# Small-matmul bursts re-ordered in a fused attention and MLP kernel, with its q/k and v loads requested earlier

One core of a Trainium2 chip (trn2). The metric is the device time of one execution in microseconds, taken from several executions per kernel; lower is better.

## The reference, cut to what matters

```python
# q, k, v: (8, 8, 576, 64). Attention per batch and head, two branches added:
q_d, k_d, v_d = means of q, k, v over 4 neighbouring positions      # 144 positions
out_up    = repeat(softmax(q_d k_d^T / 8) v_d, 4)
out_local = softmax(q k^T / 8 where |i - j| < 4) v
x = (out_up + out_local) as (4608 tokens, 512)
# then the MLP:
h = x @ w_in            # 512 -> 2048
out = (h * sigmoid(1.702 h)) @ w_out     # 2048 -> 512
```

## The kernel before

The MLP runs in nine groups of 512 tokens: 64 dense matmuls for `w_in` (`mm1`), 64 for `w_out` (`mm2`), 512 columns each. The attention of batch g+1 runs beside the dense matmuls of group g, as bursts of small matmuls at numbered positions (0 to 79, four dense matmuls per position in `mm1`, one per position from 16 on). Below, "group 1 to 6" are the six groups with the regular positions `POS`; group 0 carries batch 1 at its own positions, groups 7 and 8 carry no attention. "AV" is the product of the scores' exponentials with v; a PSUM tile is a buffer that TensorE's results go to.

```python
POS = [13, 16, 33, 42, 53, 62, 71]
# 13: scores of heads 0-3 (s_pe(0))   16: their exponentials    33: scores of heads 4-7 (s1)
# 42: AV of head pairs 0, 1           53: AV of pairs 2, 3      62, 71: transposes back

def s_pe(qd):
    st["s", qd] = scores(b, qd)      # 80 matmuls, 32x64 tiles, 60 columns, two PSUM tiles
    st["d", qd] = scores_d(b, qd)    # 24 matmuls, 144 columns, the third PSUM tile

# the third blocks of the downsampled AV: two array tiles, and a filler in the other two
blocks = [(kc, x, 0) for kc in range(3) for x in range(2)]
blocks += [(0, 0, 1), (0, 1, 1), (1, 0, 1), (2, 0, 1)]     # (0, 1, 1) is the filler

# per group, in program order; GpSimd issues q/k loads and does pooling and casts itself
load_v4(b)                           # SyncE queue
prep_qk(b, 0); pool_qk(b, 0)         # VectorE transposes, GpSimd pooling
for qd in range(NQ): load_qk(b + 1, qd)     # GpSimd queue, f32 to bf16 on the way
prep_v(b, nc.gpsimd)                 # GpSimd cast of v, needs v of batch b
load_v(b + 1)                        # SyncE queue, after the cast
prep_qk(b, 1); pool_qk(b, 1); prep_v4(b, nc.gpsimd)
```

The softmax here doesn't subtract the row's maximum and nothing guards it: scores larger than these inputs give would overflow.

## Time and profile before

| | before |
|---|---|
| device time, median (range) | 324.07 us (323.53 to 325.09) |
| span of the profiled run | 321.3 us |
| granted TensorE clock, mean | 0.999 |
| groups 1 to 6, one undisturbed group | 33.4 us |

How to read it: the chain is the work that ended last, followed back from the end of the run; the granted clock is the share of its full clock that TensorE was given. TensorE is on the chain for nearly the whole span, so every pause of TensorE is added to the time. To see a burst's cost I take the time from the last dense weight load before it to the first dense weight load after it. In this measure the six bursts of an undisturbed group take 1.683, 1.747, 1.339, 1.340, 1.073 and 1.073 us (first scores, second scores, AV, AV, transposes, transposes). What a burst takes beyond its clean time (the changed bursts have clean times of their own, 1.60, 1.67, 1.26, 1.26, 1.05 and 1.05 us) is called a stop.

### The profile page before, as it was taken

What the parts mean: (1) busy time and instruction counts of PE and PEld (TensorE: products, weight loads), DVE (VectorE), ACT (ScalarE), POOL (GpSimd) and SP (SyncE); (2) the same over time, 40 slices, a digit from 0 to 9 for tenths busy, and PEclk for the clock granted to TensorE, in tenths of its full rate; (3) what the DMA queues carried; (4) which work ended last, traced back from release to release, by engine and by line L of the source; (5) the groups of instructions that cost most, each with busy time, mean ns of one, the idle gap of its engine ahead of it and who ended that gap; (6) DMA issues with size and microseconds to landing.
All of it is one profiled execution on the core that took longest, in us unless ns stands there. A gap on an engine that the chain in (4) does not pass through costs nothing.

```text
span 321.3 us, 10981 instructions
## 1 busy us (share of the span) xinstructions
PE 314.1 (98%) x4916; PEld 158.9 (49%) x4916; DVE 135.3 (42%) x224; ACT 183.9 (57%) x317; POOL 140.0 (44%) x172
## 2 busy tenths in 40 slices
PE   8999999999999999999999999999999999999995
PEld 3764555455444455455545554455445544444444
DVE  6973627802673076605770478036811650000000
ACT  4565762667456673668365936683677466415611
POOL 8992960299009920794059603980296000000000
PEclk9999999999999999999999999999999999999999
DMA  7999999899619941895169715991360110020011
GB/s 121 114 198 210 177 122 207 159 247 253 161 43 207 196 117 67 185 215 130 65 150 215 168 37 144 213 197 46 108 106 3 69 67 2 0 98 33 2 62 68
DMA packets 63550, 40.02 MB, mean 125 GB/s; under 512 B 44048, under 2 KB 54416, under 8 KB 63504
## 3 DMA queue, kind: packets, MB, share of 16 engines
q0 software_dynamic: 18864, 14.95, 32.4%
q1 hardware_dynamic: 44496, 24.32, 31.1%
q8 instruction: 38, 0.62, 0.9%
q14 instruction: 8, 0.07, 0.1%
q10 hardware_dynamic: 144, 0.07, 0.1%
HBM read 44.83 MB, written 9.44 MB: 169 GB/s over the span
## 4 chain that ended last, share of the span: by engine, by line
PE 94%; DVE 2%; DMA 2%; issue 1%; POOL 0%; ACT 0%; DVEq 0%; POOLq 0%
PE pm L687 37%; PE pm L743 36%; PE pa L373 4%; PE pa L743 2%; PE pa L687 2%; PE pa L487 2%; PE pa L392 2%; PE pa L434 2%; PE pa L456 2%; DMA qb<-in_q_dram 2%; PE pm L758 1%; PE pm L816 1%; DVE y L473 1%; PE pa L573 1%; PE pa L497 0%
## 5 line engine op out<-in xcount | busy, mean ns | idle before, releaser
L743 PE MATMUL pm<-w_out_bf,gT 128*128 128x512 bf16 x528 | 121.7, 380 | 0.0
L687 PE MATMUL pm<-xT,w_in_bf 128*128 128x512 bf16 x544 | 121.1, 379 | 0.0
L698 ACT ACTIVATE gT<-pm 128x512 bf16<-128x512 f32 x136 | 81.0, 598 | 44.6 <-PE pm L687 44.6
L687 PEld LDWEIGHTS <-w_in_bf 128*128 128x128 bf16 x576 | 55.6, 98 | 66.8 <-issue 0.4
L743 PEld LDWEIGHTS <-gT 128*128 128x128 bf16 x560 | 51.6, 98 | 59.1 <-issue 0.2
L417 DVE TENSOR_TENSOR es<-es,mask 128x600 bf16<-128x600 bf16 x28 | 20.2, 736 | 84.8 <-ACT es L403 83.9
L294 POOL TENSOR_TENSOR pq<-kT 128x576 f32<-128x576 bf16 x14 | 16.3, 1161 | 88.4 <-DVE kT L276 88.4
L728 ACT ACTIVATE osb<-pm 128x512 f32<-128x512 f32 (+2 forms) x35 | 20.8, 594 | 40.0 <-PE pm L743 35.6
L599 ACT COPY od<-pa 128x384 f32<-128x384 f32 (+1 forms) x56 | 18.5, 412 | 32.9 <-DVE y L473 15.0
L473 DVE TENSOR_TENSOR y<-pa,rc 128x896 bf16<-128x896 f32 x28 | 30.6, 1091 | 1.0
L620 DVE TENSOR_TENSOR xT<-pa,od 128x570 bf16<-128x570 f32 x28 | 21.1, 753 | 12.2 <-ACT od L599 10.8
L730 DVE TENSOR_SCALAR osb<-pm 128x128 f32<-128x128 f32 x1 | 0.3, 292 | 55.3 <-ACT osb L728 55.3
L314 POOL TENSOR_TENSOR v<-v 112x512 f32<-112x512 f32 x18 | 22.8, 1266 | 0.0
L276 DVE STREAM_TRANSPOSE kT<-kb 128x576 f32<-128x576 f32 x16 | 20.0, 1249 | 4.1 <-DMA kb<-in_k_dram 3.9
L403 ACT ACTIVATE es<-pa 128x600 bf16<-128x600 f32 x32 | 19.7, 667 | 2.7 <-PE pa L373 2.4
L276 DVE STREAM_TRANSPOSE qT<-qb 128x576 f32<-128x576 f32 x16 | 19.9, 1242 | 0.4
L230 POOL DMA_DIRECT2D vb<-in_v_dram x20 | 13.7, 696 | 6.6 <-DMA w_in_bf<-in_moe_w_in_dram 4.4
L409 ACT ACTIVATE ed<-pa 128x864 bf16<-128x864 f32 x16 | 14.4, 897 | 2.0 <-PE pa L392 1.8
L373 PEld LDWEIGHTS <-kT 32*64 32x64 bf16 x1280 | 11.9, 104 | 7.0 <-issue 5.9
L294 POOL TENSOR_TENSOR pq<-qT 128x576 f32<-128x576 bf16 x13 | 14.9, 1146 | 0.0
L472 DVE RECIPROCAL rc<-pa 128x14 f32<-128x14 f32 x28 | 6.7, 240 | 18.2 <-PE pa L456 18.2
L317 POOL TENSOR_TENSOR vd<-v 112x256 bf16<-112x256 f32 x18 | 13.7, 759 | 1.4
(98 smaller groups left out, 268.8 us busy)
## 6 DMA issues: line engine op xcount, KB each, us to landing
out_dram<-osb SPq DMA_DIRECT2D x35, 256.0 KB, 2.1
vf<-in_v_dram SPq DMA_DIRECT2D x60, 128.0 KB, 5.2
v<-in_v_dram SPq DMA_DIRECT2D x36, 192.0 KB, 4.6
kb<-in_k_dram POOLq DMA_DIRECT2D x16, 288.0 KB, 6.7
qb<-in_q_dram POOLq DMA_DIRECT2D x16, 288.0 KB, 8.4
w_out_bf<-in_moe_w_out_dram POOLq DMA_DIRECT2D x4, 512.0 KB, 18.2
vb<-in_v_dram POOLq DMA_DIRECT2D x20, 64.0 KB, 5.1
w_in_bf<-in_moe_w_in_dram POOLq DMA_DIRECT2D x2, 512.0 KB, 6.3
```

Source lines behind the costliest of these rows:

```text
L276: nc.vector.transpose(out=t32.rearrange("p (i c) -> p c i", c=18), in_=store[b, qd].bitcast(FP32).rearrange("p (c d) -> p c d", c=18),)
L294: eng.tensor_tensor(out=t1, in0=sv[:, :, 0:2, :], in1=sv[:, :, 2:4, :], op=ALU.add)
L314: eng.tensor_tensor(out=t1[0:112], in0=x[:, :, 0:2, :], in1=x[:, :, 2:4, :], op=ALU.add)
L373: nc.tensor.matmul(sp[r // 2][64 * par : 64 * par + 64, r % 2, 60 * i : 60 * i + 60], lhsT=kT[b, qd][rows, k0 : k0 + 64, a], rhs=qT[b, qd] ...
L403: nc.scalar.activation(out=es[2 * qd + u][:, :, 0:300], in_=sp[u][:, :, 0:300], func=AF.Exp, scale=inv_sqrt_d,)
L417: nc.vector.tensor_tensor(out=ev, in0=ev, in1=mask, op=ALU.mult)
L473: nc.vector.tensor_tensor(out=y[:, xs], in0=ov[:, :, :, 0:D], in1=rc[:, xs].to_broadcast([128, n, 7, D]), op=ALU.mult,)
L620: eng.tensor_tensor(out=sub(xT[hp], t0 + 3, (57, 2), (114, 5), (1, 57)), in0=sub(x, 3, (509, 2), (57, 5), (1, 57)), in1=sub(od, 3, (57, 2) ...
L687: nc.tensor.matmul(acc, lhsT=w_in_bf[:, dmc, ffc * 128 : (ffc + 1) * 128], rhs=xT[dmc][:, g * TG : g * TG + TG], start=(dmc == 0), stop=(d ...
L698: nc.scalar.activation(out=gT[:, ffc, :], in_=acc, func=AF.Silu, scale=GELU_SCALE)
L728: eng.activation(out=osb, in_=ap, func=AF.Copy, scale=1.0 / GELU_SCALE)
L743: nc.tensor.matmul(ops[t], lhsT=gT[:, ffc, t * 128 : (t + 1) * 128], rhs=w_out_bf[:, ffc, :], start=(ffc == 0), stop=(ffc == n_ffc - 1),)
```

## The change

Its intent: let long and short score matmuls use the array's tiles side by side, balance the tiles in AV and transposes, drop the fillers, and ask for q/k and v of the next batch as early as GpSimd can. The diff is cut; the comments are mine.

```diff
+    def scores_mixed(b, qd):
+        sp = [ps_tile(), ps_tile()]
+        sd = ps_tile()
+        ahead = {2 * kc: (lambda kc=kc: scores_d(b, qd, sd, [kc])) for kc in range(3)}
+        return scores(b, qd, sp=sp, ahead=ahead), sd      # 8 long ones ahead of i = 0, 2, 4
...
+    def av(b, hps, ns):                  # both pairs of a burst together
+        for kc in range(3):
+            for hp, o in zip(hps, os):
+                av_down(b, hp, o, [(kc, hp % 2, 1)])     # pair 0 on two tiles, pair 1 on the others
+        for hp, o in zip(hps, os):
+            av_local(b, hp, o)
+            av_down(b, hp, o, [(kc, x, 0) for kc in range(3) for x in range(2)])
-        blocks += [(0, 0, 1), (0, 1, 1), (1, 0, 1), (2, 0, 1)]
... (transposes in the same way)
-    POS = [13, 16, 33, 42, 53, 62, 71]
-    POS_0 = [16, 18, 27, 48, 52, 57, 66, 70, 75]
+    POS = [13, 16, 35, 42, 53, 62, 71]
+    POS_0 = [16, 18, 30, 48, 52, 57, 66, 70, 75]
...
-            prep_qk(b, 0)
-            pool_qk(b, 0)
             if b + 1 < B:
                 for qd in range(NQ):
                     load_qk(b + 1, qd)
             prep_v(b, nc.gpsimd)
             if b + 1 < B:
                 load_v(b + 1)
+            prep_qk(b, 0)
+            pool_qk(b, 0)
             prep_qk(b, 1)
```

More of the change, by code (lines that the diff above doesn't have):

```diff
@@ L360, in bar_others, with scores @@
             )
-    def scores(b, qd, barred=False, sp=None):
+    def scores(b, qd, barred=False, sp=None, ahead={}):
         sp = sp or [ps_tile(), ps_tile()]
@@ L366, in scores @@
         for i in range(5):
+            if i in ahead:
+                ahead[i]()
             for a in range(2):
@@ L382, in scores, with scores_d @@
         return sp
-    def scores_d(b, qd, sd=None):
+    def scores_d(b, qd, sd=None, kcs=range(3)):
         sd = sd or ps_tile()
         bank = banks(sd)
-        for kc in range(3):
+        for kc in kcs:
             for a in range(2):
@@ L417, in mask_local @@
             nc.vector.tensor_tensor(out=ev, in0=ev, in1=mask, op=ALU.mult)
-    def av(b, hp, n=None):
-        o = ps_tile(n)
-        av_local(b, hp, o)
-        av_down(b, hp, o)
-        return o
+    def av(b, hps, ns):
+        os = [ps_tile(n) for n in ns]
+        for kc in range(3):
[4 more added lines that the diff above has]
+            av_down(b, hp, o, [(kc, x, 0) for kc in range(3) for x in range(2)])
+        return os
     def banks(t):
@@ L440, in av_local, with av_down @@
                     )
-    def av_down(b, hp, o):
+    def av_down(b, hp, o, blocks):
         Ed, vd, u, o = eds[hp // 2], vds[b % 2], hp % 2, banks(o)
-        blocks = [(kc, x, 0) for kc in range(3) for x in range(2)]
-        blocks += [(0, 0, 1), (0, 1, 1), (1, 0, 1), (2, 0, 1)]
-        if True:
-            for kc, x, c2 in blocks:
-                for j in range(2):
-                    pos = j if x == 0 else 1 - j
-                    c0 = 65 * (5 + c2)
-                    q0 = SD * kc + 48 * (min(x + c2, 1) + x)
-                    last = x == c2 == 1
-                    if last:
-                        q0 = 0
-                    nc.tensor.matmul(
-                        o[j][64 * pos : 64 * pos + 64, c0 : c0 + 65],
-                        lhsT=Ed[64 * j : 64 * j + 48, u, q0 : q0 + 64],
-                        rhs=vd[64 * j : 64 * j + 48, kc, hp, :],
-                        start=(kc == 0), stop=(kc == 2 or last),
-                        tile_position=(64 * j, 64 * pos),
-                    )
+        for kc, x, c2 in blocks:
+            for j in range(2):
+                pos = j if x == 0 else 1 - j
+                c0 = 65 * (5 + c2)
+                q0 = SD * kc + 48 * (1 + hp % 2 if c2 else (2 - hp % 2) * x)
+                nc.tensor.matmul(
+                    o[j][64 * pos : 64 * pos + 64, c0 : c0 + 65],
+                    lhsT=Ed[64 * j : 64 * j + 48, u, q0 : q0 + 64],
+                    rhs=vd[64 * j : 64 * j + 48, kc, hp, :],
+                    start=(kc == 0), stop=(kc == 2),
+                    tile_position=(64 * j, 64 * pos),
+                )
     def normalise(o):
@@ L477, in normalise, with turn_down, turn_local @@
         return y
-    def transp(y, n=None):
-        x = ps_tile(n)
+    def turn_down(y, x, c2, xx):
+        for j in range(2):
+            pos = j if xx == 0 else 1 - j
+            nc.tensor.matmul(
+                x[64 * j : 64 * j + 64, xx, 288 + 48 * c2 : 336 + 48 * c2],
+                lhsT=y[64 * pos : 64 * pos + 48, j, 5 + c2, :],
+                rhs=ident(pos, 48, 0, 48),
+                start=True, stop=True,
+                tile_position=(64 * pos, 64 * j),
+            )
+    def turn_local(y, x):
         for i in range(5):
@@ L493, in transp @@
                     )
-        for c2, xx in ((0, 0), (0, 1), (1, 0)):
-            for j in range(2):
-                pos = j if xx == 0 else 1 - j
-                nc.tensor.matmul(
-                    x[64 * j : 64 * j + 64, xx, 288 + 48 * c2 : 336 + 48 * c2],
-                    lhsT=y[64 * pos : 64 * pos + 48, j, 5 + c2, :],
-                    rhs=ident(pos, 48, 0, 48),
-                    start=True, stop=True,
-                    tile_position=(64 * pos, 64 * j),
-                )
-        return x
+    def transp(hps, ys, ns):
+        xs = [ps_tile(n) for n in ns]
+        if len(hps) > 1:
+            for hp, y, x in zip(hps, ys, xs):
+                turn_down(y, x, 1, hp % 2)
+        for hp, y, x in zip(hps, ys, xs):
+            turn_local(y, x)
+            for xx in range(2):
+                turn_down(y, x, 0, xx)
+            if len(hps) == 1:
+                turn_down(y, x, 1, hp % 2)
+        return xs
     def av_local0(hp, o, chunks):
@@ L594, in copy_x, with copy_od @@
         nc.scalar.copy(out=xT[hp][:, t0 + 231 : t0 + S], in_=x[1][:, 0:345])
-    def copy_od(x):
+    def copy_od(hp, x):
         od = work.tile([128, S], FP32, name="od", tag="od")
-        for xx, t0, n in ((0, 0, 96), (1, 96, 48)):
+        n0 = 48 if hp % 2 else 96
+        for xx, t0, n in ((0, 0, n0), (1, n0, SD - n0)):
             nc.scalar.copy(
@@ L647, in s_pe @@
         def s_pe(qd):
-            st["s", qd] = scores(b, qd)
-            st["d", qd] = scores_d(b, qd)
+            st["s", qd], st["d", qd] = scores_mixed(b, qd)
         def s_act(qd):
@@ L665, in f @@
             def f():
-                for hp in hps:
-                    st["o", hp] = av(b, hp, slots and slots[hp % 2])
-                for hp in hps:
-                    st["y", hp] = normalise(st["o", hp])
+                ns = [slots and slots[hp % 2] for hp in hps]
+                for hp, o in zip(hps, av(b, hps, ns)):
+                    st["y", hp] = normalise(o)
             return f
@@ L673, in f @@
             def f():
-                for hp in hps:
-                    st["x", hp] = transp(st["y", hp], slots and slots[hp % 2])
-                for hp in hps:
-                    od = copy_od(st["x", hp])
-                    merge(b, hp, st["x", hp], od)
+                ns = [slots and slots[hp % 2] for hp in hps]
+                for hp, x in zip(hps, transp(hps, [st["y", hp] for hp in hps], ns)):
+                    od = copy_od(hp, x)
+                    merge(b, hp, x, od)
             return f
```

## The prediction

> **What bounds the kernel now.** I read the page first (busy shares, DMA row, chain by line), then the chain in order of time, then the timeline of TensorE inside single bursts, then the timelines of GpSimd and of the DMA queue of SyncE around the loads.
>
> ```profile
> PE 314.1 (98%) x4916; PEld 158.9 (49%) x4916; DVE 135.3 (42%) x224; ACT 183.9 (57%) x317; POOL 140.0 (44%) x172
> ...
> PEclk9999999999999999999999999999999999999999
> ...
> PE 94%; DVE 2%; DMA 2%; issue 1%; POOL 0%; ACT 0%; DVEq 0%; POOLq 0%
> ```
>
> TensorE carries 94% of the chain at full clock, and no other engine is near full. So time falls only if TensorE's own sequence gets shorter, or grows if it has to wait. The chain of one undisturbed batch (the seventh, beside the two dense products of a 512-token group):
>
> ```profile
> 229.29 11.22 PE pm L687 x52
> 240.51 0.77 PE pa L373 x79
> 241.28 0.39 PE pa L392 x23
> 241.67 2.70 PE pm L687 x12
> 244.37 3.67 PE pm L743 x17
> 248.04 0.77 PE pa L373 x80
> 248.81 0.46 PE pa L392 x24
> 249.26 2.05 PE pm L743 x9
> ...
> 257.48 0.28 PE pa L487 x20
> 257.76 0.05 PE pa L497 x6
> ```
>
> Columns are start, length, what. A dense matmul costs 11.22/52 = 0.216 us. Between dense stretches stand six bursts of small matmuls: two score bursts (0.77+0.39 = 1.16 and 0.77+0.46 = 1.22), two AV bursts (0.82 each, from 251.31 to 252.13 and from 254.61 to 255.43) and two transpose bursts (0.55, the first begun by the last two lines). Each is followed by 0.11 us extra at the first dense matmul (2.05 for 9 instead of 1.94). Sum 5.12 + 0.66 = 5.8 us of a 33.4 us group (262.68 less 229.29); the rest is 128 dense matmuls, 27.6 us. Only the 5.8 us, seven times over, is open to this change.
>
> Inside a burst, starts of successive instructions show two limits. In the score burst, after the first 35 or so that were queued, one matmul starts every 8.3 ns (240.68 to 241.07): its weight load and itself, 4.2 ns each, a supply limit. The 24 downsampled scores (144 columns) start four at a time every 63 ns: they use four of the eight 32x64 tiles, each busy for its 144 columns, a tile limit. The AV bursts start four every 30 ns at first, then at the 8.3 ns supply, with 65 ns of stragglers at the end: the third block of both pairs uses the same two tiles.
>
> In the first batches the bursts are dearer, and not for tile reasons:
>
> ```profile
> 82.90 0.25 PE L456 MATMUL pa<-vd,ed 48*64 48x65 bf16 x6 [0.25 <-issue]
> ...
> 87.17 0.29 PE L456 MATMUL pa<-vd,ed 48*64 48x65 bf16 x11 [0.45 <-issue]
> ...
> 117.84 0.28 PE L456 MATMUL pa<-vd,ed 48*64 48x65 bf16 x8 [0.28 <-issue]
> ```
>
> These lines are timeline lines of AV bursts that stop in the middle with nothing to wait for ("issue"). Counting TensorE's records, the stops at 82.9, 87.2, 117.8 and 188.3 us all fall at the same place, record 193 or 194 of a block of 256. They cost 0.44+0.64+0.47+0.24 = 1.8 us over a clean burst.
>
> **What the Trainium skill says.** "TensorE: Matmul & The Clock Gate", Part 3, has small matmuls on different tiles run concurrently, but matmuls start in strict program order; the AV burst here contradicts the second half: at 254.858 us a matmul of the second pair (L434) starts before the last two of the first pair (254.880 and 254.887), so a free tile passes a busy one. "TensorEngine Tiling (Array Packing)", Key Properties: changing tiling mode drains the array; the trace agrees (the 0.11 us at each burst's end). "Runtime: NRT & Kernel Launch", Instruction fetch mechanics: instructions come in 16 KiB blocks of 256 by DMA, which is "mostly hidden"; here the instruction queue moved 38 packets for 0.62 MB and the block edges match the stops, so it is not hidden in a burst. "DMA: Bandwidth & Descriptors", Queues, rings and completion order: engines take rows in turn by packet, so other queues delay the fetch. Here a fetch starts some 0.8 us after it is due with quiet DMA, and 2.2 to 3.7 us late while q/k loads run (for instance 106.3 to 109.7 us); from its start to use takes another 2.5 us.
>
> **The change part by part.**
> 1. Mixed scores. Instruction count is the same, but 24 tile-limited matmuls can run beside 80 supply-limited ones. Supply of all: 0.64 us for the 80 scores + 24 x 8.3 ns = 0.84, plus the 0.15 us tail = about 1.0 to 1.05 instead of 1.16 to 1.22. I take 0.15 saved, 14 bursts (seven batches): 2.1 us. The last chunk of eight long ones stands before the last 16 scores, so its tile time (126 ns) is nearly covered.
> 2. AV. Per pair of heads the filler goes: 80 to 76 matmuls in a burst, 4 x 8.3 = 33 ns, and the third blocks, now on complementary tiles and in front, take the straggling 60 ns away. 0.09 per burst; in the batch of the first group the next transposes wait for VectorE's normalisation anyway (0.19 at 50.24), so 12 bursts: 1.1 us.
> 3. Transposes: same 52, better alternation. About 0.02 x 12: 0.2 us.
> Sum of gains: 3.4 us.
> 4. Positions. The second score burst moves two dense matmuls later because it now needs its third PSUM tile at once; that tile is freed at 214.94 by the exponential, and the burst would start at 210.98 + 19 x 0.216 = 215.08: no wait, but only 0.14 us to spare. AV follows after 7 instead of 9 dense matmuls: both its tiles need the two local exponentials, 1.23 us behind the scores' end, against 1.6 us available. No cost expected.
> 5. Requests moved. GpSimd then issues q/k right after the pooling of the previous batch, during the second dense product, where the second scores and the AV bursts stand, and no longer in the first dense product. The cast of v moves ahead of the pooling too.
>
> **The rivals.** (a) Fetch stalls grow. The q/k traffic (6.6 to 9.5 us per batch now, 102.9 to 109.5 us in the third) moves over scores, AV and AV, which use 548 instructions in some 6.6 us. A fetch that falls due in the second score burst would come about 5.5 us later (3 + 2.5), while the next block edge in the first AV burst is reached after about 3. Averaged over where an edge can fall that is about 1.2 us for each of the four groups whose successor still loads: 4.8 instead of 1.8, so +3. Against it: I know the load's start only to a microsecond, and fewer instructions (16 less per batch) move every edge. I count half, +1.5.
> (b) Pooling behind the cast. Two lines of GpSimd's timeline and one of SyncE's queue:
>
> ```profile
> 64.86 0.67 POOL L297 TENSOR_TENSOR qdT<-pq 128x288 bf16<-128x288 f32 x1
> ...
> 67.90 2.35 POOL L308 CAST vb<-vf 128x2560 bf16<-128x2560 f32 x1
> ```
>
> ```profile
> 51.97 10.45 SPq L219 DMA_DIRECT2D vf<-in_v_dram  x10
> ```
>
> Today the first half of the pooling of batch 2 ends at 65.5, and the first scores of that group start at 71.3: 5.8 us to spare. After the change GpSimd runs the cast first, and the cast needs v of batch 2, requested at 52 and landed at 64.7 now. The q/k of batch 3, then requested at 52 as well, would share the engines with it (in the mix at 70 to 77 us the q/k queue takes 0.71 of them and the other 0.37). I work out v landing at 66.5 to 68.5, the cast done 2.4 later and the pooling 3.7 later still: 72.6 to 74.6 against scores due at about 70.8. That is a wait of 2 to 4 us, once, in the first full group; in later groups the cast finds its data long landed and the wait is nil. Against it: the two positions that were moved (33 to 35, 27 to 30) look tuned on a trace, and whoever tuned them would have seen such a gap. I count 1.2 us.
> (c) No overlap in the score burst. If matmuls started strictly in order, as the skill's page has it, a chunk of eight long ones would hold up the scores behind it for its 126 ns and mixing would gain nothing: 2.1 us less. The AV starts quoted above speak against it.
> (d) The 0.14 us to spare for the third PSUM tile is not there: 0.1 us in each of seven batches, 0.7 at most.
>
> **The sum and the range.** 324.1 - 3.4 (bursts) + 1.5 (a) + 1.2 (b) = **323.4 us**. If (a) and (b) do not come at all and the present 1.8 us of stops shrink, it is 319 to 320.5; with the bursts at their supply limit in full, 318.5. If both come in full (+3 and +3), 326.5 to 327; with (c) besides, 328.5. So **318.5 to 328.5 us** for 8 times in 10. Faster by over 2% means under 317.6: more than the bursts can give, chance 0.04. Slower by over 2% means over 330.6: all rivals in full and more, 0.05. Within 2%: 0.91.
>
> **What would show it right or wrong.** Mixed score bursts in an undisturbed group (the last two with attention) of 1.00 to 1.08 us from first small matmul to first dense one, with L373 and L392 alternating; 1.15 or more would make step 1 wrong. AV bursts of 0.72 to 0.76 with 76 matmuls; transposes of 0.52 to 0.55. For (a): stops marked "issue" in the AV bursts of groups two to five, 256 records apart, longer than 0.5 us, and q/k traffic running there; their sum against 1.8. For (b): TensorE idle just before the first score burst of the first full group, released by GpSimd's pooling (qdT), with the cast ending after 68. If both are absent the time is near 320.5 and my two charges were wrong; if the groups without loads do not get about 0.55 us shorter each than 33.4, the gains were.

## The result, and the profile after

| | before | after |
|---|---|---|
| device time, median (range) | 324.07 us (323.53 to 325.09) | 340.11 us (339.12 to 344.59) |
| ratio of fast runs, 95% interval | | 1.050 (1.045 to 1.055) |
| span, profiled run | 321.3 us | 337.4 us |
| six clean bursts of a group | 8.26 us | 7.89 us |
| stops in bursts, groups 1 to 6 | 2.2 us | 15.5 us |

Ratios here are the mean time of one kernel's fast runs over that of the other's in the same rounds, so not quite the ratio of the medians quoted. The change made the kernel 5% slower: far outside the predicted range, though the bursts themselves did get shorter.

The page of the changed kernel, to be set against the lines of the page shown in the prediction:

```profile
PE 309.4 (92%) x4806; PEld 158.5 (47%) x4860; DVE 135.1 (40%) x224; ACT 183.9 (55%) x317; POOL 139.7 (41%) x172
...
PEclk9999999999999999999699989999999999999999
...
PE 72%; DMA 10%; issue 6%; POOL 6%; SPq 4%; DVE 1%; ACT 0%; POOLq 0%; DVEq 0%
```

TensorE fell from 94% to 72% of the chain; DMA, GpSimd and "issue" (waiting for nothing the profile shows) took the rest. This is not 22% of lost time: at 75.2 us TensorE waits for GpSimd, which had waited for a load, and from there back to the start of the kernel the chain runs through loads and GpSimd, not through TensorE, though TensorE was busy then as well. The granted clock has a dip in the twentieth slice and a smaller one in the twenty-fourth.

**One wait for data.** First the before, then the after: the first score burst of group 1 in TensorE's timeline, and GpSimd's timeline ahead of it.

```profile
71.26 0.95 PE L373 MATMUL pa<-qT,kT 32*64 32x60 bf16 x80
```

```profile
75.18 0.26 PE L394 MATMUL pa<-qdT,kdT 32*64 32x144 bf16 x4 [3.21 <-POOL qdT L297]
```

```profile
69.12 2.32 POOL L308 CAST vb<-vf 128x2560 bf16<-128x2560 f32 x1 [14.49 <-DMA vf<-in_v_dram]
...
74.47 0.66 POOL L297 TENSOR_TENSOR qdT<-pq 128x288 bf16<-128x288 f32 x1
```

The brackets give the idle time ahead and what ended it. GpSimd stood idle for 14.5 us ahead of the cast, because v of batch 2 landed only at 68.3 us (64.7 before; the end of its last packet), and the pooling that the scores need came after the cast.

**Long stops with nothing to wait for.** The first AV burst of group 3. First the first and the last line of its counterpart before, which has no stop:

```profile
150.71 0.35 PE L434 MATMUL pa<-vb,es 64*64 64x65 bf16 x20
...
151.23 0.37 PE L456 MATMUL pa<-vd,ed 48*64 48x65 bf16 x19
```

Then the changed kernel:

```profile
156.37 0.25 PE L461 MATMUL pa<-vd,ed 48*64 48x65 bf16 x7
160.05 0.27 PE L461 MATMUL pa<-vd,ed 48*64 48x65 bf16 x5 [3.42 <-issue]
```

Seven matmuls, 3.4 us of nothing, and on. The DMA view of the stretch from 150.5 us to 157.4 us names all queues that moved anything:

```profile
q0 software_dynamic: 538, 1.13, 99.3%
```

and of the next 1.6 us, to 159.0:

```profile
q1 hardware_dynamic: 136, 0.25, 41.7%
q0 software_dynamic: 37, 0.05, 17.8%
q8 instruction: 1, 0.02, 3.7%
```

Columns are packets, MB, and share of the 16 engines' time; q0 is GpSimd's queue, q1 SyncE's, and q8 brings TensorE's instructions (38 packets in a run, as many as its stream has block edges). While q/k (q0) fills the engines, no instruction packet is moved; the block (256 instructions, one packet) came as that traffic died down (157.6 to 158.6 us), and TensorE went on 1.5 us after it. The block edge that this packet follows was passed before 154 us (at about 151.4, by counting weight loads, two instructions each). The instruction queue was not alone in this: a store that SyncE issued at 154.05 us on q1 moved no packet before 157.4 us either. In the same stretch before (148 to 152 us), with q1 at 49% of the engines and no q/k, the packet was moved:

```profile
q8 instruction: 1, 0.02, 2.6%
```

**A slower clock behind the stop.** TensorE in stretches around it; columns are length, busy time with count, granted clock, DMA share and GB/s:

```profile
151.00:157.00 6.00, 5.46 (x130) 1.00 1.06 174
157.00:160.00 3.00, 0.00 (x0) 0.88 0.50 137
160.00:162.00 2.00, 1.62 (x71) 0.50 0.03 8
162.00:164.00 2.00, 2.00 (x6) 0.50 0.00 0
164.00:166.00 2.00, 2.00 (x9) 0.50 0.30 113
166.00:168.00 2.00, 1.84 (x82) 0.98 0.09 27
```

After this stop (3.6 us between weight loads) the clock was granted at one half for 6.8 us, and after the stop of 3.0 us in group 4 for 3.4 us. The length of a pause does not settle it: after the wait of 3.2 us in group 1 the clock stayed at 1.00. Dense matmuls of groups 1 to 6 took 3.2 us more in sum for this.

Where the time went, groups 1 to 6, from the first score burst on (189.8 us before, 205.3 after): clean bursts -2.2, stops and waits +13.2 (15.5 less 2.2), slower dense matmuls +3.2, and one more pause of 1 us in a dense stretch. The start of the kernel adds 0.6, the last two groups nothing. In the table below, the 0.5 and 0.4 of the second AV bursts of groups 3 and 4 are bursts run at the halved clock, not interruptions.

| stop beyond the clean burst, us | before | after |
|---|---|---|
| group 1: first scores | 0.1 | 3.3 |
| group 1: AV, AV | 0.4, 0.6 | 1.5, 0 |
| group 2: AV, AV, transposes | 0.5, 0, 0 | 0, 1.1, 0.6 |
| group 3: AV, AV | 0, 0 | 4.0, 0.5 |
| group 4: AV, AV | 0, 0.2 | 3.0, 0.4 |
| group 5: AV, AV | 0, 0 | 0, 0 |
| group 6: AV, AV | 0, 0 | 0.9, 0 |

### The profile page after: what moved, and what is told of

It is laid out like the page before. It is cut to its first block, busy times and chain, and to the rows that moved or that the text cites. A ratio compares the mean times of both kernels' runs of the same rounds, so it can differ in the third digit from the quotient of the medians.

```text
span 337.4 us, 10815 instructions
## 1 busy us (share of the span) xinstructions
PE 309.4 (92%) x4806; PEld 158.5 (47%) x4860; DVE 135.1 (40%) x224; ACT 183.9 (55%) x317; POOL 139.7 (41%) x172
## 4 chain that ended last, share of the span: by engine, by line
PE 72%; DMA 10%; issue 6%; POOL 6%; SPq 4%; DVE 1%; ACT 0%; POOLq 0%; DVEq 0%
PE pm L758 32%; PE pm L702 29%; DMA qb<-in_q_dram 7%; SPq L219 4%; DMA w_out_bf<-in_moe_w_out_dram 3%; PE pa L375 2%; PE pa L461 2%; PE pa L394 2%; POOL vb L230 2%; PE pa L446 1%; PE pa L502 1%; PE pm L773 1%; POOL pq L294 1%; DMA vf<-in_v_dram 1%; PE pa L487 1%
## 5 line engine op out<-in xcount | busy, mean ns | idle before, releaser
L758 PE MATMUL pm<-w_out_bf,gT 128*128 128x512 bf16 x493 | 118.3, 388 | 6.5 <-issue 6.3
L702 PE MATMUL pm<-xT,w_in_bf 128*128 128x512 bf16 x527 | 119.7, 379 | 0.7
L702 PEld LDWEIGHTS <-w_in_bf 128*128 128x128 bf16 x576 | 55.6, 98 | 66.5 <-issue 0.4
L758 PEld LDWEIGHTS <-gT 128*128 128x128 bf16 x560 | 52.5, 99 | 63.2 <-issue 7.0
L308 POOL CAST vb<-vf 128x2560 bf16<-128x2560 f32 x6 | 14.1, 2352 | 15.8 <-DMA vf<-in_v_dram 15.8
L375 PE MATMUL pa<-qT,kT 32*64 32x60 bf16 x1280 | 17.5, 199 | 1.1 <-DVE qT L276 1.1
L394 PE MATMUL pa<-qdT,kdT 32*64 32x144 bf16 x384 | 15.2, 231 | 3.2 <-POOL qdT L297 3.2
L461 PE MATMUL pa<-vd,ed 48*64 48x65 bf16 x504 | 12.3, 198 | 5.6 <-issue 5.6
L375 PEld LDWEIGHTS <-kT 32*64 32x64 bf16 x1280 | 15.8, 103 | 1.6 <-issue 1.3
```

The costliest lines, as they stand in the source:

```text
L375: nc.tensor.matmul(sp[r // 2][64 * par : 64 * par + 64, r % 2, 60 * i : 60 * i + 60], lhsT=kT[b, qd][rows, k0 : k0 + 64, a], rhs=qT[b, qd] ...
L394: nc.tensor.matmul(bank[r // 2][64 * j : 64 * j + 64, SD * kc : SD * kc + SD], lhsT=kdT[qd][rows, 48 * kc : 48 * kc + 64, a], rhs=qdT[b, q ...
L702: nc.tensor.matmul(acc, lhsT=w_in_bf[:, dmc, ffc * 128 : (ffc + 1) * 128], rhs=xT[dmc][:, g * TG : g * TG + TG], start=(dmc == 0), stop=(d ...
L758: nc.tensor.matmul(ops[t], lhsT=gT[:, ffc, t * 128 : (t + 1) * 128], rhs=w_out_bf[:, ffc, :], start=(ffc == 0), stop=(ffc == n_ffc - 1),)
```

## The experiments

My theory after the result: the moved q/k requests put 8 us of traffic over the second scores and the AV bursts, where TensorE uses up a block of 256 instructions in less time than a fetch now takes; the cast ahead of the pooling adds one wait. The main rival: the denser bursts and the new positions themselves cause the stops.

### Take the requests back, keep the bursts

```diff
 (the changed kernel)
+            prep_qk(b, 0)
+            pool_qk(b, 0)
             load_qk(b + 1, ...); prep_v(b, nc.gpsimd); load_v(b + 1)
-            prep_qk(b, 0)
-            pool_qk(b, 0)
```

> The changed kernel with the requests back in their old order (q/k after the first pooling, v after that); bursts and positions as changed, so TensorE's instruction stream is the same instruction for instruction. Theory (the moved requests cause the loss: q/k traffic over the AV bursts delays the instruction fetch, and the cast holds up the pooling once): about 321.5 us (320.5 to 323), stops inside bursts of 1 to 3 us in all, no stop over 1.2 us, granted clock 0.99 or more. Rival (the shorter, denser bursts and the new positions themselves run out of instructions or out of PSUM tiles): 330 us or more with stops of 3 us in AV bursts at the same instructions.

Measured: 324.45 us median (323.31 to 329.54), 0.998 of before (0.991 to 1.005). With the same instructions for TensorE in the same order, 5% is gone: the new order on GpSimd (requests and cast) is the cause. The number expected was too good by 3 us. The profiled run counts as slow (over 1.5% above the fastest of its kernel; clock 0.984, halved for 6.8 us from 21.9 us and for 3.4 us from 90.1 us), so its stops (1.9, 1.0 and 0.7 us in the first AV bursts of groups 1, 4 and 6) are not compared in size; they lie at the same block edges as after the change. Four fast runs had clock 1.00.

### The requests alone, on the bursts of before

> The kernel before with the new request order alone; bursts and positions as before. Theory: 334 us (330 to 339): a wait of about 3 us before the first scores of the first full group, and long fetch stops in AV bursts, at other places than in the changed kernel because the block edges lie elsewhere; clock below 0.99. Rival (the bursts themselves cause it): 324 to 327 us, only the one wait.

Measured: 337.64 us (335.23 to 344.97), ratio 1.036 (1.028 to 1.045), clock 0.985. As the theory has it. The ratio is below the 1.050 of the whole change, though the profiled spans are nearly equal (337.0 and 337.4 us); the runs don't settle what the rest is. Two lines of its TensorE timeline, group 1's downsampled scores and group 2's first AV burst:

```profile
76.34 0.93 PE L392 MATMUL pa<-qdT,kdT 32*64 32x144 bf16 x24 [4.50 <-POOL qdT L297]
```

```profile
128.02 0.38 PE L456 MATMUL pa<-vd,ed 48*64 48x65 bf16 x8 [3.01 <-issue]
```

The old bursts stop about as long as the new ones in all (15.2 us of stops and waits in groups 1 to 6, 15.5 after the change), at other places. So the mixing is not needed for the loss.

### v ahead, q/k not; and q/k ahead, v not

```diff
 (v_early: the changed kernel)          (qk_early: the changed kernel)
   prep_v; load_v                         load_qk
   prep_qk(b, 0); pool_qk(b, 0)           prep_qk(b, 0); pool_qk(b, 0)
   load_qk                                prep_v; load_v
```

> The changed kernel with q/k requested after the first pooling as before, but cast and request of v still ahead of the pooling. Theory (it is the q/k traffic, not v): 322 us (320.5 to 324), the cast ends before 68 and the first scores of the first full group wait for less than 0.5 us, stops of 1 to 3 us in all. Rival (v ahead of the pooling is what hurts, by traffic or by order): over 330 us.

> The changed kernel with only q/k requested ahead; cast and request of v after the first pooling as before. Theory: the wait of 3.3 us before the first scores of the first full group goes, the fetch stops stay: 336.5 us (333 to 340), with at least 8 us of stops in bursts and a clock below 0.99. Rival (v is what hurts): below 326 us.

Measured: with v ahead 326.36 us (325.06 to 330.11), ratio 1.003 (0.996 to 1.010); with q/k ahead 336.91 (332.02 to 340.61), ratio 1.027 (1.016 to 1.037). The q/k requests carry most of the loss, with 12.0 us of stops in the profiled run. How much is less sure: two of the four runs with q/k ahead count as fast, and the interval lies on both sides of 1.02. A run counts as slow by its time, which long stops lengthen too, so this ratio may be low. The number for v was a miss: 326 where 322 was expected, and 7.0 us of stops. That v ahead costs something by itself is likely but not shown: its interval overlaps that of the run with both in the old place. In both runs the wait of 3.3 us before group 1's first scores was gone (their first score burst there takes 1.61 and 1.60 us, a clean one). So that wait needs both: the cast ahead of the pooling, and q/k traffic that delays v.

### The same change with 128 instructions more at the start

If the stops belong to edges of instruction blocks, they must move when the count moves, though no burst, wait or load changes. TensorE waits for its first data anyway, so tiny matmuls there cost little.

```diff
     warm(4)
+    pad = pm_tile()
+    pm_tile()
+    for _ in range(64):
+        nc.tensor.matmul(pad[:, 0:16], lhsT=zero16[:, 0:128], rhs=zero16[:, 0:16], start=True, stop=True)
```

> The changed kernel with 64 tiny matmuls (128 instructions) added at the very start, where TensorE waits for its first data, so that every block edge moves by half a block against the bursts while all else stays. Fetch theory: the long stops leave the first AV bursts of the fourth and sixth-from-start groups (groups 4 and 6) and come in those of groups 2 and 3, again at the same remainder of 256 in the new count, 3 to 4 us each; total time between 330 and 345. Rival (stops are caused by data or PSUM waits of those bursts): the stops stay in groups 1, 3, 4 and 6 as they are.

Measured: 341.42 us (one run, state unknown). First AV bursts of groups 2 and 3:

```profile
128.12 0.33 PE L446 MATMUL pa<-vb,es 64*64 64x65 bf16 x8 [3.48 <-issue]
```

```profile
167.13 0.23 PE L461 MATMUL pa<-vd,ed 48*64 48x65 bf16 x5 [2.77 <-issue]
```

The stops left the first AV bursts of groups 1, 4 and 6 (all three now at the clean 1.26 us) and came in groups 2 (4.0 beyond clean) and 5 (1.3), and in the second AV bursts of groups 1 (1.2) and 4 (1.1); group 3 kept one (3.0), but after the 71st matmul of the burst where it had been after the 7th. The wait ahead of group 1's first scores stayed (3.0), as a wait for data should. Counted as two instructions for each weight load, every interruption of 1 us or more inside an AV burst of groups 1 to 6 lies at 184 to 190 modulo 256, in all kernels here. The rival (data or PSUM waits of those bursts) is out for the long stops.

### Half of the q/k traffic ahead

```diff
 (the changed kernel, v in its old place)
+            load_qk(b + 1, 0)
             prep_qk(b, 0); pool_qk(b, 0)
+            load_qk(b + 1, 1)
```

> The changed kernel with v in its old place and only the first half of the q/k requests ahead (the second half after the first pooling, as before): the early q/k traffic lasts 4 us and no longer 8. If a fetch waits until that traffic is over, it now ends before or just after the second scores begin, the fetch is there about 2.5 us later, and the stops in the AV bursts fall below 1 us each: 1.000 to 1.010 of the kernel before, where the run with all q/k ahead had 1.027 and a median of 337. If the delay comes from the early request as such (its issue on GpSimd, its descriptors), not from how long the traffic lasts, the stops stay: 1.02 or more.

Measured: 332.34 us (328.28 to 334.15), ratio 1.028 (1.020 to 1.036), but only two of its four runs count as fast. This is the other outcome (1.02 or more), so the ratio does not support that the length of the traffic decides. In the profiled run (328.28, the fastest of its four) the stops are 8.6 us in all, against 12.0 with all q/k ahead, and none reaches 3 us; the clock stayed at 1.00. Group 4's first AV burst:

```profile
189.98 0.28 PE L446 MATMUL pa<-vb,es 64*64 64x65 bf16 x9 [1.88 <-issue]
```

Its stop was 4.1 us with all q/k ahead (gap between weight loads), 2.1 here, and group 1's also fell (2.3 to 1.4). But in group 2 the stop grew from 1.1 to 1.4 us, and in group 3 from 1.3 in the second AV burst to 2.0 in the first: that longer early traffic makes each stop longer is not shown. My number ("below 1 us each") was a miss. In group 4 the half in front still covered the fetch: by count the edge was passed at 185.1 us, q/k packets ran from 185.6 to 190.6 us, and the instruction packet came at 187.7 us. The ratio is no lower than with all q/k ahead; these intervals do not separate the two.

### Does the mixing pay where the requests are in their old place?

```diff
 even_gaps: bursts_only with    POS = [13, 16, 35, 44, 53, 62, 71]
 fine_mix:  even_gaps with six chunks of four long matmuls, ahead of (i, a) =
            (0,0) (0,1) (1,1) (2,0) (3,0) (3,1)
 av_only:   scores not mixed, POS and POS_0 of before; AV and transposes as changed
```

> The bursts of the change, the old request order, and the first AV burst two dense matmuls later (position 44 for 42), so that the gaps between the second scores, AV, AV and transposes are 9, 9, 9 and 9 dense matmuls and no longer 7, 11, 9, 9. Fetch theory: a block of 256 instructions lasts 0.43 us longer across the second scores and the first AV, so the stops that the run with the old request order had there (1.9, 1.0 and 0.7 us in a run in the slow state) shrink by about 0.4 each: 0.985 to 0.995 of the kernel before. Rival (those stops have another cause, such as a late exponential): no change against the run with the old order, about 0.998.

> As even_gaps, and the downsampled scores go in six chunks of four, with at least eight ordinary scores between two chunks, where the change has three chunks of eight. If the mixed burst's shortfall (0.08 us gained for 0.15 predicted) comes from the second four of a chunk waiting for their tiles' first four, the score burst shortens by another 0.05 to 0.10 us: 1.55 us from last dense to first dense weight load where the change has 1.60, and the run is 0.7 to 1.4 us faster than even_gaps. If the burst is limited by the supply of instructions, it stays at 1.60 and 1.67.

> The AV and transpose parts of the change alone: scores unmixed, old positions, old request order. The bursts should show AV 1.263 and transposes 1.051 from last dense to first dense weight load (0.077 and 0.023 less than before), scores unchanged at 1.68 and 1.75: 1.2 us less, plus or minus what the moved block edges do to the stops (about 1 us either way): 0.992 to 1.000 of the kernel before.

Measured on one chip: even_gaps 324.10 us (321.38 to 327.97), 0.998 (0.993 to 1.002); fine_mix 323.65 (322.99 to 324.39), 0.999 (0.995 to 1.003); av_only 321.12 (320.31 to 321.94), 0.992 (0.987 to 0.997).

In clean bursts every part does what it should: mixed scores 1.60 and 1.67 us (1.68 and 1.75 before), finer mixing 1.54 and 1.61, AV 1.263 (1.340), transposes 1.051 (1.073). The finer mixing gains another 0.06 per burst, so the three chunks of eight did cost tile time. But in the run of the whole kernel the mixing's gain does not show: the profiled runs had stops of 2.9 us (even_gaps) and 4.9 us (fine_mix), where av_only had 1.0 and before 2.2. The wider gap did not help as expected: the first AV burst of group 4 stopped for 1.4 us, and 0.998 is the rival's number (no change). That fine_mix is faster than even_gaps, as expected, is not shown: their intervals overlap. Why mixed scores run with more stops even in the old request order is open; shorter bursts leave less time per block, but 0.08 us is small against these stops.

### A version meant to beat both

```diff
 (fine_mix with the positions of before, and in s_pe:)
+            if qd == 0: mixed in six chunks
+            else:       scores, then scores_d, as before
```

> A version meant to beat both: old request order and old positions, AV and transposes as changed, and the first score burst of each batch mixed in six chunks of four; the second one unmixed, so that it needs its third tile late. First score bursts 1.54 us (1.68 before), second 1.75, AV 1.263, transposes 1.051: 1.0 us less than the run with AV and transposes alone, with the same block edges: about 320.2 us, 0.985 to 0.992 of the kernel before. Rival (stops eat it, as in the runs with both scores mixed): 0.993 or more.

Measured: 320.75 us (319.98 to 321.63), 0.9905 (0.986 to 0.995). It beats both kernels, by 1% against before. Of the expected 1.0 us over av_only nothing is sure: 0.9905 and 0.992 were measured on different chips and their intervals overlap; its profiled run had 1.9 us of stops in groups 1 to 6.

## Why the prediction was wrong

- **Step 1 (mixed scores), half size.** Predicted 0.15 us per burst, measured 0.08. Two tile-limited fours per chunk still hold the scores back; chunks of four gave 0.14. The mechanism (free tiles pass busy ones) holds: rival (c) would have given nothing.
- **Steps 2 and 3, right.** AV 0.077 for 0.09, transposes 0.022 for 0.02.
- **Step 4 (positions), right as far as seen:** no wait for the third PSUM tile stands out, and the second scores have no stops beyond 0.02 us after the change.
- **Rival (b), right in size, wrongly discounted.** v landed at 68.3 (predicted 66.5 to 68.5), the cast ended 2.3 later, the pooling at 75.1, and TensorE waited 3.2 us (predicted 2 to 4). I counted 1.2 because moved positions "look tuned on a trace". That was a guess about the author against a sum worked out from the trace.
- **Rival (a), the step that failed.** The direction was right: stops at block edges in the AV bursts. The sum's term was "4.8 instead of 1.8, so +3", of which I counted half. Measured: 12 us of stops in AV and transposes (15.5 less the 3.3 of the pooling and 0.2 in other scores), so +10, and a pause of 1 us between dense matmuls. Groups 2 to 4 have 9.6 us of it, 3.2 for each, where the sum had 1.2. Two things in the term failed. First, the averaging over where an edge can fall, though edges can be counted. Group 4 went nearly as the term has one hit: an edge in the second scores (193.6 us by count), TensorE going on 5.8 us after it (5.5 in the sum), the next edge 2.8 us after it (3 in the sum), so a stop of 3.0. Second, the lateness "2.2 to 3.7 us": from edge to packet it was 3.5 us in group 4 and 4.0 in group 2, but in group 3 the edge was passed near the start of the q/k traffic and the packet started only at 157.6 us, as that traffic died down: over 3.5 us late by the latest possible due time, some 6 by count. Late fetches did not always come at the end: in group 1 one came at 91.2 us, with q/k packets from 86.5 to 94.0 us.
- **Two stops that (a) does not cover.** Group 1's first AV (1.5 us) waited for a packet of 84.5 to 86.2 us, before that q/k traffic began, and group 6's (0.9) had no q/k traffic at all. The same bursts stop with the requests in their old place (1.9 and 0.7 us in bursts_only). Their cause is open.
- **Missing altogether: the clock.** After the two longest stops the granted clock was halved for 6.8 and 3.4 us; +3.2 us in dense matmuls and 0.9 in AV bursts (counted above as stops) in the profiled run. Nothing in my sum stood for it.
- **The range.** It summed "in full" cases at +3 and +3. With the measured terms the sum is: bursts -2.2, stops +10, pooling wait +3.3, clock +3.2, pause and start +1.6: near +16, as measured.

## What to carry to other kernels

A request that is "free" because its issuing engine is idle is not free if its traffic lies over a stretch that uses instructions fast: look for pauses marked "issue" at a fixed remainder of the instruction count, and keep long loads beside the dense stretches. On a kernel bound by TensorE, a pause of a few microseconds can cost more than its length: after the stops of 3.0 and 3.6 us here the granted clock was halved for 3.4 and 6.8 us, though not after a wait of 3.2 us. And a rival that was worked out from the trace should be counted in full, not weighed down by the thought that somebody must have noticed.

## What the Trainium skill lacked or had wrong

The pages are those of the Trainium skill.

- "Runtime: NRT & Kernel Launch", Instruction fetch mechanics, calls the cost of crossing a 16 KiB block "mostly hidden". In bursts of small matmuls it is not: 1.8 us of AV stops before, 11 us in AV and transposes after the change, at 184 to 190 modulo 256 of TensorE's instructions (two for each weight load).
- "DMA: Bandwidth & Descriptors", Queues, rings and completion order, has engines take their rows in turn by packet. In group 3 an instruction packet whose edge was passed before 154 us, and a store issued at 154.05 us, moved nothing before 157.4 us, while q/k traffic filled the engines to 99%; in group 1 a packet did come in the midst of such traffic (at 91.2 us). The page says nothing of what that does to the fetch.
- "TensorE: Matmul & The Clock Gate", Part 3, The mechanism, calls matmuls monotone in start and end, with no reordering. On different tiles the records show otherwise. Each chunk of the mixed burst has eight long matmuls (L394) ahead of the short ones (L375) in the program; in the changed kernel's first scores of group 2, TensorE's timeline shows six short ones started ahead of the fifth long one:

```profile
110.87 0.26 PE L394 MATMUL pa<-qdT,kdT 32*64 32x144 bf16 x4
110.90 0.25 PE L375 MATMUL pa<-qT,kT 32*64 32x60 bf16 x6
110.96 0.23 PE L394 MATMUL pa<-qdT,kdT 32*64 32x144 bf16 x1
```

Mixing shortened the burst by 0.08 us, and by 0.14 in chunks of four.
